# Gelu of 18 FFN tiles straight from PSUM and the attention normalisation on GpSimd, in a fused attention and FFN kernel

## The chip, the cores and the metric

The kernel runs on one core of a Trainium2 chip. The metric is the device time of one execution in microseconds (us). Engines are named as the profile names them: PE is TensorE's matmul, PEld its weight load, DVE VectorE, ACT ScalarE, POOL GpSimd, SP SyncE, which issues nearly all DMAs.

## The reference

The input x has 2048 rows of 512 in bf16. It is normalised per row (no gain or shift); on the result run a multi-query attention with 32 heads of width 16 that share one K and one V, and an FFN of width 1792. Their sum and x are the output.

```python
xn = (x - mean(x)) / sqrt(var(x) + 1e-5)
q = (xn @ wq) as 32 heads of 16;  k = xn @ wk;  v = xn @ wv      # one k and v for all heads
attn = (softmax(q k^T * 16**-0.5) @ v) @ wo
ffn = gelu_tanh(xn @ w1 + b1) @ w2 + b2                          # 512 -> 1792 -> 512
out = x + attn + ffn
```

## The kernel before

**Tiles and units.** The queries are cut into four blocks of 512 (`tb`), the heads into eight groups of four. A score tile is one head, one block of 128 keys and 512 queries: 128 x 512 fp32, one PSUM bank. There are 2048 of them, taken three at a time as 683 *units* `u`. `scores(u)` (L947) writes the unit's three tiles with three matmuls, side by side in PE's rows, into one half of six banks: banks 0 to 2 for even units, 3 to 5 for odd ones. Bank 6 (`pO`) holds the running sum of P x V, bank 7 (`pM`) whatever else is projected.

**Two ways to an exponential.** `DTAB` is a string with one letter for each unit and says which of its tiles are *D tiles*. The other tiles go to ACT: `exp(u)` (L970) writes E in bf16, one instruction for the one, two or three tiles of the unit, and one matmul sums each tile into `pO` (L1014, `E,V`). D tiles go to DVE: a first pass `p1` (L1001) reads the bank and writes the bits of an approximate exponential as int16 to `Dt`; then further passes make shifted copies, over a batch of several D tiles at a time (`close_batch`, L1047 on DVE), and one pass in place per tile on POOL (L1044, 128 x 512 int16), which the planner gives back to DVE where it finds no place. Five matmuls then sum a D tile (L1014, `Dt,V`). The column matmuls use 32 of PE's columns, so that four run side by side.

**FFN.** `h_mm` projects one of the 14 tiles of h of a query block into `pM` with 16 column matmuls (L661, `xnT,w_sb`), and DVE evacuates it with the bias b1 to `ub` (even blocks) or `x_sb` (odd ones) (L1150). Gelu needs another table on ACT than the exponential, so it is done in two batches: after units 182 and 512, for two query blocks at a time. `gelu` (L1162) issues four instructions of seven tiles each, 128 x 3584 in place in SBUF, between two table loads. The units near a batch are mostly D tiles. `y_mm` (L661, `w_sb,ub` and `w_sb,x_sb`) multiplies with w2 afterwards.

**Attention output.** After the last tile of a head group `o_evac` copies `pO` to `Of` on DVE (L1059). DMAs reorder it to `OfP`, the sums go through a reciprocal on DVE (L1071) and through DRAM to `rbP`, spread over the rows, and for each pair of groups DVE multiplies `OfP` by `rbP` into `oTp`, 128 x 512 from two fp32 inputs (L1086). `wo_mm` reads `oTp`.

**The order.** All instructions are recorded with a cost (`occ`) and a latency (`lat`). A planner at build time, `Prog.schedule`, lists them on the engines by those costs; what comes out is a fixed order for each engine, and the waits are semaphores. `HP`, `YP` and `QK` say at which unit an h tile, an output tile or a query projection is offered. The planner knows that a pass of POOL should not run beside DVE's `lock` instructions (passes of Dt, L1086): it starts POOL's together with a long DVE instruction that is not locked, and the constants `PL_START`, `PL_OCC`, `PL_LAT`, `PL_FREE`, `PL_SEM` say how. Where PE would idle too long in a stretch it adds filler matmuls (L1318).

Of the kernel before, what the change touches and what calls it, by code (L numbers as in the profile page):

```python
# [7 lines left out]
ALU = mybir.AluOpType  # L8
# [50 lines left out]
CLOSE = "otABX"  # L59
DTAB = "t2t22t00202t..22tt..022.to00.t22t00200..o.t..20222o.o2.tot22.2t.t2222tt22..2o222t2..o202o02tt2.o.2.t0.t202.2.20t0toto.2..0ot.t2..ot0o2t02t.2222o.0t...o0ot2020o2.2t0.02.t00.02.20o002..xxXaoto.02oot.0to2tt.0too0.ot0tot.o0o020t0o0.tt20.t22.o0tto..2t2to220oo.22t0.2ooo.o2t2o.0ot0o.t02t022.to0..oot.2t2t.o0002ot.0.2tto.0tt2.02t0.202t.2t.oo.ot0.00t.t0o0.0o0o..o0o22o2.00.t0tot2.0o2.2o.t2o2o.tt22o.0t.0oo.2ot2t2.o0.t0t20to2.2t0t.tt2t.002tt.oo.o0oooo0.2o0o0.t00t2ot2.0t0tt0.oA.o..020tt2t02..t0000...2o..02ot0020o.t2t...00XbXttto200t.tt0o22tt..0t0t222.o2o2.t2t20.t0t0.t0t00t2o.0tt2tot.t000202t2t.o.0to20.0.2o22t0o.2t00o0t0..t02o0.0o.o0ooto.t2t0to.2oo0o222o0022o00.2t.2..t0t2.2t.tttt2.2.to.o.."  # L60
YF = 664
# [11 lines left out]
HP = ((14.33,26.29,49.54,147.27,14,38.77,51.6,14,34.61,92.18,56.17,130.88,103.7,49),(108.69,82.59,66.39,104.08,133,93.7,109.35,162.93,173.36,139,171.29,159.02,133,137.17),(308.62,328.89,290.1,325,306.98,336.81,316.24,310.73,293.91,381.46,369.7,349,374.48,453.6),(475,473.57,427,468.62,459.3,464.72,451,455.66,491.16,486.09,482.33,480.6,464.72,461.37))  # L73
YP = ((195.26,184.23,228.93,254.61),(353.39,411.43,387.54,421),(516,530.79,566.23,553.42),(600.53,607,655.32,660.47))
GU = ((182, (0, 1)), (512, (2, 3)))
FG = 7
UB2 = 2
# [26 lines left out]
class _Op:  # L104
    __slots__ = ("eng", "fn", "deps", "sdeps", "stream", "amt", "need", "ticket", "waits", "clock", "occ", "lat",
                 "allow", "kind", "tag", "nun", "outs", "rel", "lock", "pm", "rdy", "start", "end", "vis", "idx", "done", "due", "real")


class Prog:
# [18 lines left out]

    def add(self, eng, fn, r=(), w=(), acc=None, dma=None, occ=0.1, lat=0.15, allow=1.0, kind=None, tag=None, after=(), due=None, lock=False):
        op = _Op()  # L130
        op.lock = lock
        op.eng, op.fn = eng, fn
# [46 lines left out]
        for o in after:  # L179
            sdeps.setdefault(id(o), (o, True))  # L180
        if self.in_chain:
# [42 lines left out]
    def schedule(self):  # L224
# [30 lines left out]
        started = {}  # L255
        opened = None
        lockend, gate, prev = 0.0, None, None
        s_seen = False
# [7 lines left out]
        while left:  # L266
# [71 lines left out]
            else:  # L338
# [26 lines left out]
                if e == "dve" and op.kind == "pl":  # L365
                    ready["pool"].remove(op)
                    ready["dve"].append(op)
                    op.eng = op.stream = "dve"
                    op.kind, op.occ, op.lat = "post", vcost(TBW, 4), 0.16
                if e == "dve":  # L370
# [86 lines left out]
    def settle(self):  # L457
        free = {e: 0.0 for e, _ in self.SECTIONS}
        mode, cg, pend = None, [0.0] * 4, 0.0
        for op in self.ops:  # L460
            occ = op.occ + EXP_OCC * (op.kind == "exp")
            lat = {"exp": EXP_LAT, "S": S_REAL, "fill": 0.0}.get(op.kind)
            lat = op.lat if lat is None else lat
            t = max([free[op.eng]] + [o.real for o in op.deps])
# [13 lines left out]
            free[op.eng] = max(free[op.eng], end)  # L478
            op.real = t + occ + lat

    def emit(self):
# [45 lines left out]
def bass_parallel_sum__grouped_kv_mqa__dense_activation_gelu__prompt_kernel(  # L527
# [33 lines left out]
    with ExitStack() as es:  # L561
# [80 lines left out]

        def dve(fn, r=(), w=(), n=TBW, mode=1, allow=1.0, lat=0.16, **kw):
            return add("dve", fn, r, w, occ=vcost(n, mode), lat=lat, allow=allow, **kw)

# [3 lines left out]
        def mm(o, l, rh, start, stop, r=(), w=(), tp=None, skip=False, occ=0.216, allow=1.5, **ak):  # L649
            kw = {}  # L650
            if tp is not None:
                kw["tile_position"] = tp
            if skip:
                kw["skip_group_check"] = True
            return add("pe", lambda e: e.matmul(o, l, rh, start=start, stop=stop, **kw), r, w, occ=occ, lat=0.23,  # L655
                       allow=allow, **ak)

        def mm4(o, l, rh, start, stop, r=(), w=(), allow=1.5, **ak):
            for j in range(4):
                c = slice(32 * j, 32 * j + 32)  # L660
                add("pe", lambda e, c=c, j=j: e.matmul(o[c, :], l[:, c], rh, start=start, stop=stop,  # L661
                                                       tile_position=(0, 32 * j)),
                    r, [(k, j) for k in w] + [k for k in w if k != B(7)], occ=0.216, lat=0.23, allow=allow, kind="side", tag=(None, j), **ak)

# [266 lines left out]
        exps = []  # L931

        def scores(u):
            ts = list(range(3 * u, min(3 * u + 3, NTILE)))
            x = u % 2
            pieces, r = [], []
# [17 lines left out]
        def exp(u):  # L954
            ts = list(range(3 * u, min(3 * u + 3, NTILE)))
            x = u % 2
            at_ = [i for i, t in enumerate(ts) if not is_d[t]]
# [55 lines left out]
        def pv_mm(gg, j, v, kt, rhs, r):  # L1013
            add("pe", lambda e, a, b: e.matmul(pO[32 * j:32 * j + 32, :], V1[:, v, kt, :], rhs, start=a, stop=b,  # L1014
                                               tile_position=(0, 32 * j)),
                r=r + [("V", v, 0 if kt < NVA else NVA)], acc="O", occ=0.216, lat=0.23,
                allow=4.0 if gg < NTB * NGR - 1 or kt < NT - 4 else -5.0, kind="pv", tag=(gg, j))

        def close_batch():
# [18 lines left out]
            for o, i, nb, k in SPL_STEPS:  # L1038
                def keys(b):
                    return [(("D", base[b + m > 0] + q), b + m) for m in range(nb) for q in range(n)]  # L1040
                if o == i:
                    for q in range(n):
                        d = Dt[:, slot(o) + q, :]
                        add("pool", lambda e, d=d, k=k: e.tensor_scalar(d, d, 1.0, float(k), ALU.mult, ALU.add),  # L1044
                            [], [(("D", base[o > 0] + q), o)], occ=PL_OCC, lat=PL_LAT, allow=PL_DUE, kind="pl", lock=True)
                else:
# [10 lines left out]
        def o_evac(gg):  # L1057
# [25 lines left out]
            if h or end:  # L1083
                n = 64 if end else P
                keys = [(k, s, hh, j) for k in ("OfP", "rbP") for hh in range(h + 1) for j in range(HG)]
                onorm[gg - h] = onorm[gg] = dve(lambda e: e.tensor_tensor(oTp[0:n, sl, :], OfP[0:n, s, :], rbP[0:n, s, :], ALU.mult),  # L1086
                                                r=keys, w=[("oTp", sl)] + pre.pop(sl, []), allow=3.0, lock=True)

# [57 lines left out]
        def h_mm(tb, ft, ev=EV_ALLOW):  # L1146
            for d in range(DT):
# [3 lines left out]
                r=["b1T"], w=M4 + [ukey(tb, ft)], n=TBW + 57, allow=ev)  # L1151

        gelu_after = {}

        def gelu(tbs, u):
            parts = [(tb, f0) for tb in tbs for f0 in range(0, FT, FG)]
            hold = exps[u - 3:u + 1]
            for n, (tb, f0) in enumerate(parts):
                uu = ubs[tb % 2][:, f0:f0 + FG, :]
                uk = [ukey(tb, f) for f in range(f0, min(FT, f0 + FG))]  # L1160
                load = 1.35 * (n == 0) + 1.35 * (n == len(parts) - 1)
                o = act(lambda e, uu=uu: e.activation(uu, uu, ACT.Gelu_apprx_tanh), r=uk, w=uk, n=len(uk) * TBW + 1200 * load + 40,  # L1162
                        kind="gelu", due=0.0, after=hold)
                hold = [o]
# [7 lines left out]
        def wo_mm(tb, i, ps, start=False, bk=7, al=1.5):  # L1172
            for n, p in enumerate(ps):
# [3 lines left out]
                mm4(bank(bk), oTp[:, pp % NPR, i * P:(i + 1) * P], wop[:, p, :], start and n == 0, False,  # L1177
                   r=[("oTp", pp % NPR), "wop"], w=[B(bk)], allow=al)

# [53 lines left out]
        for tb in range(NTB):  # L1233
# [6 lines left out]
            for ft in range(FT):  # L1240
                at(HP[tb][ft], lambda tb=tb, ft=ft: h_mm(tb, ft), 0.66)
            if tb + 1 < NTB:
# [16 lines left out]
        for t in range(NTILE):  # L1259
            if is_d[t]:  # L1260
                first, n = (t, 1) if n == 0 else (first, n + 1)
                if n == KB or last_d[t // TPG] == t or (DTAB[t // 3] in CLOSE and not any(is_d[t + 1:t // 3 * 3 + 3])):
                    bsize[first], n = n, 0

        scores(0)
        scores(1)
        for u in range(NU):
            ts = list(range(3 * u, min(3 * u + 3, NTILE)))
            exp(u)
            if u + 2 < NU:  # L1270
                scores(u + 2)
            for t in ts:
# [12 lines left out]
            if batch and len(batch) == size[0]:  # L1285
                close_batch()
            for gu, tbs in GU:
                if u == gu:
                    gelu(tbs, u)
            n0 = len(pr.ops)  # L1290
# [66 lines left out]
```

## Time and profile before

| | us |
|---|---|
| median of 3 runs | 750.98 (750.9 to 751.15) |
| profiled execution | 750.71 |
| its span, first to last instruction | 749.0 |
| DVE busy | 736.1 |
| ACT busy | 733.2 |
| PE busy | 732.8 |
| POOL busy | 364.4 |

A row of the grouped views has the line, engine, operation, out<-in by the program's names, shapes and the count; behind the bar the time in which one of the group ran, and the mean length of one in ns; behind the second bar the engine's idle time before them. A timeline row has the start in the span, the length, and the count of equal instructions that it merges. A row of stretches has the stretch, its length, and each engine's busy time with its instructions in brackets, then the granted clock, the DMA share and GB/s.

### The profile page before, as it was taken

The page shows a single profiled execution, that of the slowest core. Times are in us where ns is not written, and L with a number is a line of the kernel's source. Part 1 is how long each engine was busy: PE and PEld are TensorE (multiplying, and loading weights), DVE is VectorE, ACT ScalarE, POOL GpSimd, SP SyncE. Part 2 cuts the span into 40 slices and gives each one's busy share as a digit, 9 for nine tenths or more (in the row PEclk, how much of TensorE's full clock was granted, in tenths as well). Part 3 has the DMA queues.
Part 4 walks back from the last instruction along what each step waited for, and adds up shares of the span by engine and source line. Part 5 has one row for each costly group of instructions (what it writes and reads, how often), then busy time and mean ns, then how long its engine had stood idle before and what let it go on. Part 6 is the DMA issues. An engine that isn't in the chain of part 4 may idle for free.

```text
span 749.0 us, 21922 instructions
## 1 busy us (share of the span) xinstructions
PE 732.8 (98%) x9046; PEld 228.2 (30%) x9046; DVE 736.1 (98%) x1436; ACT 733.2 (98%) x744; POOL 364.4 (49%) x506
## 2 busy tenths in 40 slices
PE   7999999999999999999999999999999999999998
PEld 4323222222233323232222222332233333322223
DVE  8899999999999999999999999999999999999996
ACT  8999999999999999999999999999999999999995
POOL 5443654343523576554546555553452466454441
PEclk9999999999999999999999999999999999999999
DMA  9200100000011011100101010100100101010101
GB/s 315 61 15 17 32 9 17 24 11 21 6 36 25 9 39 30 24 23 16 26 13 28 17 38 19 29 24 16 25 15 22 40 6 41 23 39 10 25 22 37
DMA packets 32077, 23.34 MB, mean 31 GB/s; under 512 B 16369, under 2 KB 27498, under 8 KB 31978
## 3 DMA queue, kind: packets, MB, share of 16 engines
q1 hardware_dynamic: 30922, 21.90, 10.9%
q8 instruction: 72, 1.18, 0.7%
q14 instruction: 27, 0.22, 0.1%
q10 hardware_dynamic: 1056, 0.03, 0.1%
HBM read 13.08 MB, written 2.35 MB: 21 GB/s over the span
## 4 chain that ended last, share of the span: by engine, by line
PE 40%; DVE 30%; ACT 28%; DMA 0%; issue 0%; SPq 0%
ACT E L970 28%; PE pAll L1014 19%; DVE Dt L1001 13%; PE pAll L947 13%; DVE Dt L1047 10%; PE pAll L661 7%; DVE x_sb L1150 2%; DVE stats L748 1%; DVE Dt L1044 1%; DVE Of L1059 1%; PE pAll L655 1%; DMA x_sb<-in_A_x_dram 0%; DVE oTp L1086 0%; DVE qp L1122 0%; DVE x_sb L1196 0%
## 5 line engine op out<-in xcount | busy, mean ns | idle before, releaser
L970 ACT ACTIVATE E<-pAll 128x1024 bf16<-128x1024 f32 (+1 forms) x678 | 682.4, 1226 | 1.7 <-PE pAll L947 1.2
L1044 POOL TENSOR_SCALAR Dt<-Dt 128x512 int16<-128x512 int16 x451 | 348.2, 772 | 360.6 <-DVE Dt L1047 143.8
L1014 PE MATMUL pAll<-Dt,V 128*32 128x512 bf16 x2775 | 421.8, 383 | 0.6 <-DVE Dt L1047 0.2
L1001 DVE TENSOR_SCALAR Dt<-pAll 128x512 int16<-128x512 f32 (+1 forms) x542 | 364.1, 688 | 1.0 <-PE pAll L947 0.8
L1047 DVE TENSOR_SCALAR Dt<-Dt 128x1024 int16<-128x1024 int16 (+7 forms) x548 | 288.0, 551 | 0.2
L1014 PE MATMUL pAll<-E,V 128*32 128x512 bf16 x1493 | 284.8, 385 | 0.2
L947 PE MATMUL pAll<-QT,KT 32*128 32x512 bf16 x2048 | 267.2, 384 | 6.2 <-ACT E L970 2.1
L947 PEld LDWEIGHTS pAll<-QT,KT 32*128 32x128 bf16 x2048 | 67.3, 91 | 279.5 <-ACT E L970 251.4
L1014 PEld LDWEIGHTS pAll<-Dt,V 128*32 128x32 bf16 x2775 | 110.9, 94 | 119.4 <-issue 72.0
L661 PE MATMUL pAll<-xnT,w_sb 128*32 128x512 bf16 x896 | 122.2, 383 | 0.4 <-DVE x_sb L1150 0.3
L1014 PEld LDWEIGHTS pAll<-E,V 128*32 128x32 bf16 x1493 | 65.9, 94 | 47.5 <-issue 34.7
L661 PE MATMUL pAll<-w_sb,x_sb 128*32 128x512 bf16 x448 | 69.3, 383 | 0.0
L661 PE MATMUL pAll<-w_sb,ub 128*32 128x512 bf16 x448 | 69.3, 383 | 0.0
L661 PE MATMUL pAll<-wop,oTp 128*32 128x512 bf16 x256 | 49.5, 383 | 0.0
L661 PEld LDWEIGHTS pAll<-xnT,w_sb 128*32 128x32 bf16 x896 | 32.1, 95 | 22.4 <-issue 11.8
L1044 DVE TENSOR_SCALAR Dt<-Dt 128x512 int16<-128x512 int16 x104 | 26.7, 279 | 0.0
L661 PE MATMUL pAll<-xnT,wq_sb 128*32 128x512 bf16 x256 | 22.5, 383 | 0.0
L1150 DVE TENSOR_SCALAR x_sb<-pAll,b1T 128x512 bf16<-128x512 f32 x28 | 20.6, 736 | 0.7 <-PE pAll L661 0.6
L1059 DVE COPY Of<-pAll 128x512 f32<-128x512 f32 x31 | 20.9, 674 | 0.0
L1150 DVE TENSOR_SCALAR ub<-pAll,b1T 128x512 bf16<-128x512 f32 x28 | 20.6, 736 | 0.0
L661 PEld LDWEIGHTS pAll<-w_sb,x_sb 128*32 128x32 bf16 x448 | 17.1, 94 | 8.8 <-issue 7.0
L661 PEld LDWEIGHTS pAll<-w_sb,ub 128*32 128x32 bf16 x448 | 17.6, 94 | 4.7 <-issue 2.9
(121 smaller groups left out, 254.6 us busy)
## 6 DMA issues: line engine op xcount, KB each, us to landing
OfP<-Of SPq DMA_DIRECT2D x124, 32.0 KB, 1.9
rbP<-rden_rows SPq DMA_DIRECT2D x124, 32.0 KB, 1.8
w_sb<-in_B_w_dram SPq DMA_DIRECT2D x2, 1792.0 KB, 12.7
x_sb<-in_A_x_dram SPq DMA_DIRECT2D x8, 256.0 KB, 4.3
x_sb<-in_A_x_dram SPq DMA_DIRECT2D x16, 128.0 KB, 2.2
QT<-qp SPq DMA_DIRECT2D x124, 16.0 KB, 1.8
out_dram<-x_sb SPq DMA_DIRECT2D x12, 128.0 KB, 1.7
wq_sb<-in_A_wq_dram SPq DMA_DIRECT2D x1, 512.0 KB, 6.2
```

What stands on the lines that cost most here:

```text
L655: return add("pe", lambda e: e.matmul(o, l, rh, start=start, stop=stop, **kw), r, w, occ=occ, lat=0.23, allow=allow, **ak)
L661: add("pe", lambda e, c=c, j=j: e.matmul(o[c, :], l[:, c], rh, start=start, stop=stop, tile_position=(0, 32 * j)), r, [(k, j) for k in w] ...
L748: dve(lambda e, ti=ti, c=c: e.bn_stats(stats[:, c, :], x_sb[:, ti, :]), r=[("x", ti)], w=[("st", ti)], n=511, due=land(ti) + DU["sd"])
L947: ins = e.matmul(o, l, rh, start=True, stop=True, tile_position=(q0, 0))
L970: o = act(lambda e: e.activation(E[:, s0:s0 + na, :], bank(b0, na).rearrange("p (a n) -> p a n", a=na), ACT.Exp, scale=LN2 / 128.0), w=[B( ...
L1001: op = dve(lambda e: e.tensor_scalar(Dt[:, s:s + n, :], bank(bk, n).rearrange("p (a n) -> p a n", a=n), float(127 * 128) + SPL_D, SPL_MIN, ...
L1014: add("pe", lambda e, a, b: e.matmul(pO[32 * j:32 * j + 32, :], V1[:, v, kt, :], rhs, start=a, stop=b, tile_position=(0, 32 * j)), r=r + [ ...
L1044: add("pool", lambda e, d=d, k=k: e.tensor_scalar(d, d, 1.0, float(k), ALU.mult, ALU.add), [], [(("D", base[o > 0] + q), o)], occ=PL_OCC, ...
L1047: dve(lambda e, d=view(o, nb), q=view(i, nb), k=k: e.tensor_scalar(d, q, float(k), None, ALU.add), r=keys(i), w=keys(o), n=nb * n * TBW, m ...
L1059: dve(lambda e: e.tensor_copy(Of[:, i, :], pO), w=["O", ("Of", i)], allow=0.0)
L1150: dve(lambda e: e.tensor_scalar(ubs[tb % 2][:, ft, :], pM, b1T[:, ft:ft + 1], None, ALU.add), r=["b1T"], w=M4 + [ukey(tb, ft)], n=TBW + 57 ...
```

## The change

**Gelu.** Each batch keeps its two instructions of seven tiles on `ub`. Of the 14 tiles on `x_sb`, five are evacuated by DVE as before and pass through one instruction of 128 x 2560; the other nine ("p") are projected late: their 16 matmuls write into one of the three banks that the batch's unit has freed, and ACT reads the bank, adds b1 as its bias and writes gelu to `x_sb`, 128 x 512, with no DVE instruction. The order on ACT is 7 tiles of `ub`, three p, 7 of `ub`, three p, the five of `x_sb`, three p. While the batch runs the scores of the next units use the other half of the banks alone; `half[u]` replaces `u % 2`, and the next units' scores are offered when the half's last user is through.

**Normalisation.** L1086's product is cut in two halves of 256 columns, recorded for POOL like the passes of L1044 (the planner may give one back to DVE), and `wo_mm` waits for the half that it reads.

**Constants and tables.** The planner's costs and latencies change, and the visibility of an exponential or gelu is now modelled as a chain (`A_LAG`, `A_INC`, `A_SEM`). `DTAB` is another string: 565 D tiles rather than 555. `HP` and `YP` are new; the 18 p tiles have no due unit of their own.

```diff
+ON_OCC = 0.66
-PL_LAT = 0.2
+PL_LAT = 0.06
-PL_START = -0.07
+PL_START = 0.065
-PL_FREE = 0.135
+PL_FREE = 0.06
-DTAB = "t2t22t00202t..22tt..022.to00.
...
+DTAB = "o2t00o20.20.t0t.2.o2oot..0t0o
...
-S_LAT = 0.27
-S_REAL = 0.222
-EXP_OCC = 0.0133
-EXP_LAT = 0.16
+S_LAT = 0.217
+A_LAG = 0.113
+A_INC = 0.0125
+A_SEM = 0.056
+D_LAT = 0.135
+P_LAT = 0.217
...
-GU = ((182, (0, 1)), (512, (2, 3)))
-FG = 7
+GU = tuple((u, tbs, n, (("s", tbs[0], 0, 7), ("p", tbs[1], 5), ("p", tbs[1], 6), ("p", tbs[1], 7), ("s", tbs[0], 7, 7), ("p", tbs[1], 8),
+                         ("p", tbs[1], 9), ("p", tbs[1], 10), ("s", tbs[1], 0, 5), ("p", tbs[1], 11), ("p", tbs[1], 12), ("p", tbs[1], 13)))
+           for u, tbs, n in ((182, (0, 1), 5), (512, (2, 3), 5)))
+HL_ALLOW = 0.0
...
+            if e == "act" and op.kind in ("exp", "gelu"):
+                aend = max(op.end + A_LAG, aend + op.occ + A_INC)
+                op.vis = aend + A_SEM
...
+        half = []
+        for u in range(NU):
+            near = [gu for gu, _, n, _ in GU if gu + 1 < u <= gu + n]
+            half.append(u % 2 if u < 2 else half[-1] if near else 1 - half[-1])
...
-            x = u % 2
+            x = half[u]
...
-                onorm[gg - h] = onorm[gg] = dve(lambda e: e.tensor_tensor(oTp[0:n, sl, :], OfP[0:n, s, :], rbP[0:n, s, :], ALU.mult),
-                                                r=keys, w=[("oTp", sl)] + pre.pop(sl, []), allow=3.0, lock=True)
+                first = pre.pop(sl, [])
+                for q in range(2):
+                    c = slice(q * TBW // 2, (q + 1) * TBW // 2)
+                    onorm[gg - h] = onorm[gg] = add(
+                        "pool", lambda e, c=c: e.tensor_tensor(oTp[0:n, sl, c], OfP[0:n, s, c], rbP[0:n, s, c], ALU.mult),
+                        keys, [("oTp", sl, q)] + first, occ=ON_OCC, lat=PL_LAT, allow=PL_DUE, kind="pl", lock=True,
+                        docc=vcost(TBW // 2))
...
+        def h_late(tb, ft, bk):
+            for d in range(DT):
+                mm4(bank(bk), w1_sb[:, d, ft * P:(ft + 1) * P], xnT[:, d, tb * TBW:(tb + 1) * TBW], d == 0, d == DT - 1,
+                    r=["w1"] + tr(4 * tb, 4 * tb + 4), w=[B(bk)], allow=HL_ALLOW)
...
+            late = [p for p in parts if p[0] == "p"]
+            for i, (_, tb, ft) in enumerate(late[:3]):
+                h_late(tb, ft, 3 * half[u] + i)
...
+                else:
+                    bk = 3 * half[u] + m % 3
+                    o = act(lambda e, bk=bk, tb=tb, f0=f0: e.activation(ubs[tb % 2][:, f0, :], bank(bk), ACT.Gelu_apprx_tanh, bias=b1T[:, f0:f0 + 1]),
+                            r=["b1T"], w=[B(bk), ukey(tb, f0)], n=TBW + 1200 * load, kind="gelu", due=0.0, after=hold)
+                    m += 1
+                    if m + 2 < len(late):
+                        h_late(*late[m + 2][1:], bk)
```

More of the change, by code (lines that the diff above doesn't have):

```diff
@@ L105 @@
     __slots__ = ("eng", "fn", "deps", "sdeps", "stream", "amt", "need", "ticket", "waits", "clock", "occ", "lat",
-                 "allow", "kind", "tag", "nun", "outs", "rel", "lock", "pm", "rdy", "start", "end", "vis", "idx", "done", "due", "real")
+                 "allow", "kind", "tag", "nun", "outs", "rel", "lock", "pm", "rdy", "start", "end", "vis", "idx", "done", "due", "real", "docc")
 class Prog:
@@ L179, in add @@
         for o in after:
-            sdeps.setdefault(id(o), (o, True))
+            sdeps.setdefault(id(o), (o, kind != "gelu"))
         if self.in_chain:
@@ L479, in settle @@
             op.real = t + occ + lat
+            if op.kind in ("exp", "gelu"):
+                aend = max(end + A_LAG, aend + occ + A_INC)
+                op.real = aend + A_SEM
     def emit(self):
@@ L931, in bass_parallel_sum__grouped_kv_mqa__dense_activation_gelu__prompt_kernel @@
         exps = []
+        half = []
+        for u in range(NU):
+            near = [gu for gu, _, n, _ in GU if gu + 1 < u <= gu + n]
+            half.append(u % 2 if u < 2 else half[-1] if near else 1 - half[-1])
+        after_u = {}
+        for v in range(2, NU):
+            after_u.setdefault(max(w for w in range(max(0, v - 12), v) if half[w] == half[v]), []).append(v)
         def scores(u):
             ts = list(range(3 * u, min(3 * u + 3, NTILE)))
-            x = u % 2
+            x = half[u]
             pieces, r = [], []
@@ L1151, in h_mm, with gelu @@
                 r=["b1T"], w=M4 + [ukey(tb, ft)], n=TBW + 57, allow=ev)
+        def h_late(tb, ft, bk):
+            for d in range(DT):
+                mm4(bank(bk), w1_sb[:, d, ft * P:(ft + 1) * P], xnT[:, d, tb * TBW:(tb + 1) * TBW], d == 0, d == DT - 1,
+                    r=["w1"] + tr(4 * tb, 4 * tb + 4), w=[B(bk)], allow=HL_ALLOW)
         gelu_after = {}
-        def gelu(tbs, u):
-            parts = [(tb, f0) for tb in tbs for f0 in range(0, FT, FG)]
+        def gelu(parts, u):
             hold = exps[u - 3:u + 1]
[L1158 to L1163, printed above, removed]
+            late = [p for p in parts if p[0] == "p"]
+            for i, (_, tb, ft) in enumerate(late[:3]):
+                h_late(tb, ft, 3 * half[u] + i)
+            m = 0
+            for n, (kind, tb, f0, *k) in enumerate(parts):
+                load = 1.28 * (n == 0) + 1.28 * (n == len(parts) - 1)
+                if kind == "s":
+                    uu = ubs[tb % 2][:, f0:f0 + k[0], :]
+                    uk = [ukey(tb, f) for f in range(f0, f0 + k[0])]
+                    o = act(lambda e, uu=uu: e.activation(uu, uu, ACT.Gelu_apprx_tanh), r=uk, w=uk, n=len(uk) * TBW + 1200 * load + 50,
+                            kind="gelu", due=0.0, after=hold)
+                else:
[5 more added lines that the diff above has]
+                        h_late(*late[m + 2][1:], bk)
                 hold = [o]
@@ L1240, in bass_parallel_sum__grouped_kv_mqa__dense_activation_gelu__prompt_kernel @@
             for ft in range(FT):
-                at(HP[tb][ft], lambda tb=tb, ft=ft: h_mm(tb, ft), 0.66)
+                if ("p", tb, ft) not in [p for g in GU for p in g[3]]:
+                    at(HP[tb][ft], lambda tb=tb, ft=ft: h_mm(tb, ft), 0.66)
             if tb + 1 < NTB:
@@ L1269, in bass_parallel_sum__grouped_kv_mqa__dense_activation_gelu__prompt_kernel @@
             exp(u)
-            if u + 2 < NU:
-                scores(u + 2)
+            if u not in [g[0] for g in GU]:
+                for v in after_u.get(u, ()):
+                    scores(v)
             for t in ts:
@@ L1286, in bass_parallel_sum__grouped_kv_mqa__dense_activation_gelu__prompt_kernel @@
                 close_batch()
-            for gu, tbs in GU:
+            for gu, _, _, parts in GU:
                 if u == gu:
-                    gelu(tbs, u)
+                    gelu(parts, u)
+                    for v in after_u[u]:
+                        scores(v)
             n0 = len(pr.ops)
```

39 lines of the change are left out of this document (21 added, 18 removed).

## The prediction, made before the result was known

> **What bounds the kernel now.** I read the page's busy lines first, then a stretch without the ends, then what each engine waited for, and last the groups of instructions kept apart by shape.
>
> ```profile
> span 749.0 us, 21922 instructions
> ...
> PE 732.8 (98%) x9046; PEld 228.2 (30%) x9046; DVE 736.1 (98%) x1436; ACT 733.2 (98%) x744; POOL 364.4 (49%) x506
> ```
>
> ```profile
> 25.00:725.00 700.00, 693.46 (x8585) 208.98 (x8584) 698.65 (x1338) 697.47 (x678) 345.32 (x449) 1.00 0.09 22
> ```
>
> ```profile
> DVE x_sb L1150 <- PE pAll L661: 0.6, 1, 0.6
> DVE Dt L1001 <- PE pAll L947: 0.3, 1, 0.3
> ```
>
> Between 25 and 725 us PE, DVE and ACT are all busy for over 99% of the time (columns PE, PEld, DVE, ACT, POOL) at a granted clock of 1.00, and DVE's list of waits holds 0.9 us. Busy time alone can't tell which of the three paces: instructions overlap, and a short wait hides in the tail of the one before. So I work out what each instruction adds to a full engine.
>
> ```profile
> 216.35 0.74 DVE L1150 TENSOR_SCALAR x_sb<-pAll,b1T 128x512 bf16<-128x512 f32 x1
> 217.00 0.68 DVE L1001 TENSOR_SCALAR Dt<-pAll 128x512 int16<-128x512 f32 x1
> 217.60 0.34 DVE L1071 RECIPROCAL den<-den 128x32 f32<-128x32 f32 x1
> ```
>
> ```profile
> 19.71 0.68 ACT L818 ACTIVATE KT<-pAll,krow 128x512 bf16<-128x512 f32 x1
> 20.28 0.35 ACT L829 ACTIVATE oTp<-pAll 128x224 f32<-128x224 f32 x1
> 24.09 1.02 ACT L970 ACTIVATE E<-pAll 128x1024 bf16<-128x1024 f32 x1 [0.54 <-PE pAll L947]
> ```
>
> ```profile
> L970 ACT ACTIVATE E<-pAll 128x1024 bf16<-128x1024 f32 x535 | 519.8, 1139 | 0.8 <-PE pAll L947 0.5
> ...
> L970 ACT ACTIVATE E<-pAll 128x1536 bf16<-128x1536 f32 x140 | 214.5, 1571 | 0.9 <-PE pAll L947 0.7 <-PE pAll L1014 0.2
> ...
> L970 ACT ACTIVATE E<-pAll 128x512 bf16<-128x512 f32 x3 | 1.9, 629 | 0.0
> ```
>
> On DVE the next instruction starts 0.60 us after one of 0.68, and 0.65 after one of 0.74: an instruction costs its mean less 75 ns. Over all 1436 instructions of the grouped view that gives 735.2 us, against 736.1 busy: DVE has about 1 us of hidden waits. On ACT the next starts 0.57 after one of 0.68, an overlap of 0.11. An exponential of 1024 that starts on an idle engine lasts 1.02, so 0.91 in a row; one of 1536 is longer by 1571 - 1139 = 432 ns, so 1.34, one of 512 0.48. Sum: 535 x 0.91 + 140 x 1.34 + 3 x 0.48 = 676 us, where L970's union, by the page, is 682.4: some 6 us of ACT's busy time are waits. DVE is the fullest engine; ACT is close behind.
>
> PE runs score triples between groups of four column matmuls:
>
> ```profile
> 213.69 0.39 PE L947 MATMUL pAll<-QT,KT 32*128 32x512 bf16 x3
> 214.01 0.40 PE L1014 MATMUL pAll<-Dt,V 128*32 128x512 bf16 x4
> ...
> 217.14 1.04 PE L661 MATMUL pAll<-xnT,w_sb 128*32 128x512 bf16 x13
> ```
>
> Thirteen matmuls are four groups, so a group costs (1.04 - 0.38) / 3 = 0.22 us, with 0.38 the length of one. A triple costs 0.32 until the next work, and as much again less one group before it: some 0.42.
>
> **The change part by part.** Counts are those of the two built programs. The rows for DVE, ACT and POOL:
>
> ```profile
> L1001 DVE TENSOR_SCALAR Dt<-pAll 128x512 int16<-128x512 f32 x534 | 352.2, 675 | 1.0 <-PE pAll L947 0.8
> L1044 POOL TENSOR_SCALAR Dt<-Dt 128x512 int16<-128x512 int16 x451 | 348.2, 772 | 360.6 <-DVE Dt L1047 143.8 <-PE pAll L1014 93.6 <-DVE Dt L1001 46.2
> ...
> L1047 DVE TENSOR_SCALAR Dt<-Dt 128x1024 int16<-128x1024 int16 x204 | 82.2, 414 | 0.1
> L1047 DVE TENSOR_SCALAR Dt<-Dt 128x2048 int16<-128x2048 int16 x105 | 71.2, 680 | 0.0
> ...
> L1047 DVE TENSOR_SCALAR Dt<-Dt 128x3072 int16<-128x3072 int16 x44 | 41.4, 943 | 0.0
> ...
> L1047 DVE TENSOR_SCALAR Dt<-Dt 128x512 int16<-128x512 int16 x116 | 31.0, 278 | 0.0
> L1044 DVE TENSOR_SCALAR Dt<-Dt 128x512 int16<-128x512 int16 x104 | 26.7, 279 | 0.0
> ...
> L1047 DVE TENSOR_SCALAR Dt<-Dt 128x1536 int16<-128x1536 int16 x38 | 20.9, 549 | 0.0
> ...
> L1150 DVE TENSOR_SCALAR x_sb<-pAll,b1T 128x512 bf16<-128x512 f32 x28 | 20.6, 736 | 0.7 <-PE pAll L661 0.6
> L1047 DVE TENSOR_SCALAR Dt<-Dt 128x4096 int16<-128x4096 int16 x17 | 20.6, 1209 | 0.0
> ...
> L1047 DVE TENSOR_SCALAR Dt<-Dt 128x5120 int16<-128x5120 int16 x9 | 13.3, 1480 | 0.0
> ...
> L1162 ACT ACTIVATE x_sb<-x_sb 128x3584 bf16<-128x3584 bf16 x4 | 12.7, 3183 | 1.3 <-DVE x_sb L1150 1.3
> ...
> L1086 DVE TENSOR_TENSOR oTp<-OfP,rbP 128x512 bf16<-128x512 f32 x15 | 10.1, 676 | 0.0
> ...
> L1047 DVE TENSOR_SCALAR Dt<-Dt 128x2560 int16<-128x2560 int16 x9 | 7.3, 806 | 0.0
> ...
> L903 POOL TENSOR_SCALAR V<-oTp 128x256 bf16<-128x256 f32 x5 | 4.3, 866 | 5.9 <-DVE oTp L897 5.5
> ...
> L1114 DVE TENSOR_TENSOR oT<-Of,pAll 128x256 bf16<-128x256 f32 x2 | 0.8, 422 | 1.2 <-PE pAll L1110 1.2
> ...
> L702 POOL COPY oTp<-wvk 128x256 bf16<-128x256 bf16 x1 | 0.4, 406 | 0.0
> ```
>
> DVE loses 18 evacuations of h (L1150): 18 x 0.661 = 11.9. It loses 16 normalisations (L1086) of 0.601, 9.6, and keeps three half ones that the planner left there, 3 x 0.347 (L1114's row) = 1.0: net -8.6. It gains ten tiles in the new table: nine more single first passes, and two doubles for one triple, which is one more tile and is taken as a single, 10 x 0.600 = 6.0. Their later passes are regrouped: by width, 512 +7 x 0.203, 1024 -30 x 0.339, 1536 +5 x 0.474, 2048 -15 x 0.605, 2560 +5 x 0.731, 3072 +5 x 0.868, 4096 +5 x 1.134, 5120 +5 x 1.405, together +5.2. DVE: -11.9 - 8.6 + 6.0 + 5.2 = **-9.3 us**.
>
> ACT keeps 678 exponentials with ten tiles fewer: -10 x 0.432 = -4.3. Two gelus of 3584 start 3.09 us apart:
>
> ```profile
> 212.38 6.27 ACT L1162 ACTIVATE ub<-ub 128x3584 bf16<-128x3584 bf16 x2
> ```
>
> (6.27 - 3.18). Four such on x_sb go, -12.4. Two of 2560 come, each two times 0.432 shorter: +4.5. Eighteen of 512 straight from PSUM come, which the trace does not show. The nearest rows are an exponential of 512, 0.48, and L818, 512 from PSUM with a bias per partition as here, 0.57. I take L818's: 18 x 0.57 = +10.3 (8.6 by the other). ACT: -4.3 - 12.4 + 4.5 + 10.3 = **-1.9 us**, to -3.6.
>
> PE gets 50 more sums from Dt and 10 fewer from E, ten groups or +2.2 us, and 36 fewer filler matmuls (L1318), nine groups or -2.0. These are level; the h matmuls are the same number.
>
> POOL gets 29 half normalisations of 256 columns. Bounds are 0.41 (L702, one input, bf16) and 0.87 (L903, one fp32 input). A product has two fp32 inputs, so I take 0.7, nearer to L903: +20 us, less 7 x 0.77 of tile passes, on an engine with 384 us idle. The cover is that idle time. The new cost is order: a half waits for sixteen DMA landings (OfP and rbP of two head groups), and behind it in POOL's queue stand the tile passes (L1044) for whose sums PE waits. POOL's halves are also placed beside a first pass of 0.60 on DVE; a half of 0.7 would outlast it by 0.1, so 29 x 0.1 = 3 us if DVE's next pass must wait, nothing if it need not, 29 x 0.27 = 8 at L903's length. The row for L1044 lasts 772 on average while the same pass on DVE stands at 279 and the doubles at 414, with nothing in DVE's waits: so far POOL does the waiting, and I put 0 in the sum.
> The Trainium skill, GPSIMD Engine Reference, section 3.1, gives about 2.6 cycles an element for a product of two inputs at 1.2 GHz; an estimate from that is 256 x 2.6 / 1.2 = 0.55 us plus dispatch, inside my bounds; section 4.1 calls VectorE the engine for such work. No row here shows the product.
>
> The planner's constants and due times move only the static order. No row prices them; I put 0, with what the rivals give on either side.
>
> **The sum.** If DVE alone paced, the time would be 750.71 - 9.3 = 741.4; if ACT alone did, 750.71 - 1.9 = 748.8. Both serve the tiles in turn through two sets of three banks, so a wait of one is passed on to the other, and the total of idle time is likelier to stay than either one's. Then the gain is the mean of both, 5.6, and the time 745.1. The profiled execution took 750.71 (span 749.0 plus 1.7 around it); the median of the runs is 750.98, 0.27 above. I predict 745.4.
>
> **The rivals.** *ACT paces* (748.8): DVE's relief only becomes idle time. Against it: after the change DVE still has 726 us of work by the sum above, ACT some 725 (733.2 - 6 - 1.9). *DVE paces throughout* (741.4): ACT would have to lose nearly all of its hidden waits.
>
> *ACT waits for the late h tiles* (slower). A tile read straight from a bank must have its 16 matmuls, four groups or 0.88 us, done between the release of that bank and its gelu; ACT spends 0.57 on it.
>
> ```profile
> 211.08:226.75 15.67, 15.48 (x194) 5.45 (x191) 15.67 (x23) 15.12 (x7) 3.72 (x5) 1.00 0.16 34
> ```
>
> ```profile
> 211.08:226.75 15.67, 4.72 (x52) 1.68 (x52) 1.00 0.16 34
> ```
>
> These are the first gelu batch with its two table loads, and the fillers (L1318) alone in it: 52 matmuls were idle PE. In the new order the four score visits of this batch hold 244 other matmuls, 61 groups, 13.4 us, plus 4 x 0.42, 15.1 in all. ACT's new batch is 2 x 1.28 + 2 x 3.09 + 2.2 + 9 x 0.57 = 16.1. PE thus has 1 us of slack where it had fillers. In each batch the late tiles come in threes behind gelus of 3.1, 3.1 and 2.2 us; three tiles take PE 2.6, so the last three are not covered unless PE does little else. If each of the nine waits out half of its matmuls and some 0.3 of hand-over, 9 x 0.74 x 2 batches = 13 us; the forecast's gain is gone at 2.8 per batch. Taking half of the tiles, 6.7: 745.1 + 6.7 = 751.8. Also, one set of banks serves the scores meanwhile, without alternation.
>
> *POOL's halves hold DVE's passes* (750 to 755). The price above, 8 us on DVE, undoes its relief: 750.71 - (1.3 + 1.9) / 2 = 749.1; if each half blocked DVE for 0.7 without any cover, 20 us, 755. For it: the products read fp32 and no row shows them beside DVE; against it: L1044's rows.
> The Trainium skill, SBUF — State Buffer, section Who interferes with whom, has it that whichever of POOL and a two-port VectorE pass starts first holds their shared ports to its end; by that rule this rival is right wherever a half starts first.
>
> *The change does little* (750.7): the new table may be no better packed than the old one, and its ten tiles may take the relief elsewhere.
>
> **How the numbers follow.** Forecast, 742 to 748: 0.55. ACT paces: 0.12. DVE paces: 0.10. Late tiles: 0.11. POOL holds DVE: 0.07, of which half near no change. Little: 0.05. A measurement can tell about 0.2%, 1.5 us. Faster by more: the first three, 0.77; within: 0.06; slower: 0.17. The range, 741 to 751.5, takes in both pacing cases and the mild end of the slower ones, and leaves out under 0.2.
>
> **What would show it.** Right: L1150's x_sb group at 10 and 18 gelus of about 0.68 (0.57 in a row) from pAll; DVE's busy time down by 8 to 10 with small visible waits; batches of about 16 us; POOL up by some 15 us. Wrong: ACT idle before the gelus from pAll by over 1 us per group of three; DVE's doubles well over 414 on average; POOL among the first that PE waits for; or a DVE busy time that does not fall.

## The result and the profile after

The changed kernel takes 746.92 us (746.81 to 747.11, four runs) beside 750.94 (750.81 to 751.15): a ratio of 0.9947, interval 0.9934 to 0.9959, 4.0 us or 0.5% faster. The profiled execution took 747.11, its span is 745.3, 3.7 less than before. The page's span and busy lines, the stretch from 25 to 725 us, and all that DVE and ACT visibly wait for in it:

```profile
span 745.3 us, 21947 instructions
...
PE 729.3 (98%) x9050; PEld 222.9 (30%) x9050; DVE 730.7 (98%) x1402; ACT 730.1 (98%) x760; POOL 380.7 (51%) x528
```

```profile
25.00:725.00 700.00, 692.78 (x8642) 203.95 (x8640) 697.25 (x1313) 698.32 (x697) 362.62 (x473) 1.00 0.09 23
```

```profile
DVE Dt L1022 <- PE pAll L968: 2.1, 5, 0.8
```

```profile
ACT E L991 <- PE pAll L968: 2.0, 4, 0.5
```

DVE's busy time fell by 5.4 us, ACT's by 3.1, POOL's rose by 16. ACT is now the busier of the two in the stretch, and DVE's first passes (L1022) wait for scores (L968) where they hardly did. The page's chain that ended last (shares of the span, followed back from the last instruction), first before and then after, says the same:

```profile
PE 40%; DVE 30%; ACT 28%; DMA 0%; issue 0%; SPq 0%
```

```profile
ACT 75%; PE 21%; DVE 3%; DMA 1%; issue 0%; SPq 0%
```

The groups that the change made or shortened (shapes kept apart; count, busy us, mean ns):

```profile
L1022 DVE TENSOR_SCALAR Dt<-pAll 128x512 int16<-128x512 f32 x543 | 362.1, 680 | 2.8 <-PE pAll L968 2.1
...
L1069 DVE TENSOR_SCALAR Dt<-Dt 128x1024 int16<-128x1024 int16 x174 | 71.2, 416 | 0.1
...
L1065 DVE TENSOR_SCALAR Dt<-Dt 128x512 int16<-128x512 int16 x121 | 32.0, 282 | 0.0
...
L1112 POOL TENSOR_TENSOR oTp<-OfP,rbP 128x256 bf16<-128x256 f32 x28 | 22.5, 812 | 12.7 <-DVE Dt L1069 9.2 <-DVE Dt L1022 1.6 <-DVE Of L1081 0.7
...
L1202 ACT ACTIVATE x_sb<-pAll,b1T 128x512 bf16<-128x512 f32 x18 | 11.1, 701 | 0.0
...
L1177 DVE TENSOR_SCALAR x_sb<-pAll,b1T 128x512 bf16<-128x512 f32 x10 | 7.4, 742 | 0.0
L1198 ACT ACTIVATE x_sb<-x_sb 128x2560 bf16<-128x2560 bf16 x2 | 4.7, 2366 | 0.0
```

The first gelu batch on ACT (timeline):

```profile
209.26 1.28 ACT L1198 ACT_TABLE_LOAD   x1
210.56 3.19 ACT L1198 ACTIVATE ub<-ub 128x3584 bf16<-128x3584 bf16 x1
213.66 1.82 ACT L1202 ACTIVATE x_sb<-pAll,b1T 128x512 bf16<-128x512 f32 x3
215.36 3.19 ACT L1198 ACTIVATE ub<-ub 128x3584 bf16<-128x3584 bf16 x1
218.44 1.85 ACT L1202 ACTIVATE x_sb<-pAll,b1T 128x512 bf16<-128x512 f32 x3
220.15 2.37 ACT L1198 ACTIVATE x_sb<-x_sb 128x2560 bf16<-128x2560 bf16 x1
222.38 1.87 ACT L1202 ACTIVATE x_sb<-pAll,b1T 128x512 bf16<-128x512 f32 x3
224.27 1.28 ACT L991 ACT_TABLE_LOAD   x1
225.56 4.69 ACT L991 ACTIVATE E<-pAll 128x1024 bf16<-128x1024 f32 x5
```

It runs without a visible wait from the start of the first table load to the next exponential, 16.30 us (225.56 - 209.26). The three late tiles of a group start 0.56 to 0.59 apart: (1.82 - 0.70) / 2 for the first group, (1.87 - 0.70) / 2 for the last. Before, each of the two batches had one visible wait for DVE's evacuations; after, this line of ACT's waits is gone:

```profile
ACT x_sb L1162 <- DVE x_sb L1150: 1.3, 2, 0.7
```

**A finer measure.** Since short waits hide in busy time, I took from the traces the time from each instruction's start to the next start on its engine, and subtracted the lower quartile of the same for its form; what is over 25 ns counts as a wait, the rest as work. From the first exponential to the last but one:

```
kernel         DVE work  waits    ACT work  waits
before           706.1    5.0       701.0   11.4
after            697.0    9.3       698.4   10.2
```

DVE's work fell by 9.1 and its waits rose by 4.3. ACT's work fell by 2.6, its waits by 1.2, and that sum, 3.8, is the gain. The 1.2 are the two gelu waits for evacuations (1.2 by this measure too); ACT's other waits stayed, 10.2 before and after. The measure depends somewhat on where the stretch is cut and how forms are grouped: taken otherwise, DVE's work falls by 8.4 and ACT's by 3.1, and the waits come out up to 0.5 us different. Where a run has shortened exponentials, most of them have a wait right behind them, so their form's lower quartile is taken from the kernels without them; by the run's own quartile ACT's waits there would come out some 9 us lower.

**Where in the span it is gained.** The start of the scores of a unit in the two traces, and how many more D tiles the new table has had up to there:

| unit | start before, us | lead of the changed kernel, us | more D tiles so far |
|---|---|---|---|
| 0 | 24 | -0.4 (behind) | 0 |
| 180 | 207 | 0.7 | 4 |
| 200 | 240 | 1.4 | 7 |
| 340 | 380 | 1.0 | 5 |
| 480 | 520 | 0.8 | 2 |
| 520 | 576 | 4.3 | 11 |
| 680 | 736 | 3.6 | 10 |

The lead does not grow steadily with DVE's relief. It grows where the new table takes tiles from ACT, above all around the second gelu batch, and shrinks a little where it gives tiles back. That fits ACT as the pace, but it is read from two traces and was not tested by a run.

### The profile page after: what moved, and what is told of

Read it like the earlier page. It is cut to its first block, busy times and chain, and to the rows that moved or that the text cites. A ratio compares the mean times of both kernels' runs of the same rounds, so it can differ in the third digit from the quotient of the medians.

```text
span 745.3 us, 21947 instructions
## 1 busy us (share of the span) xinstructions
PE 729.3 (98%) x9050; PEld 222.9 (30%) x9050; DVE 730.7 (98%) x1402; ACT 730.1 (98%) x760; POOL 380.7 (51%) x528
## 4 chain that ended last, share of the span: by engine, by line
ACT 75%; PE 21%; DVE 3%; DMA 1%; issue 0%; SPq 0%
ACT E L991 70%; PE pAll L1035 10%; PE pAll L968 7%; PE pAll L674 4%; ACT ub L1198 2%; ACT x_sb L1202 1%; DVE Dt L1022 1%; PE pAll L668 1%; DVE stats L761 1%; ACT x_sb L1198 1%; DMA x_sb<-in_A_x_dram 1%; DVE Dt L1069 0%; ACT L991 0%; ACT L1198 0%; PE pAll L812 0%; ACT xnT L817 0%
## 5 line engine op out<-in xcount | busy, mean ns | idle before, releaser
L1065 POOL TENSOR_SCALAR Dt<-Dt 128x512 int16<-128x512 int16 x444 | 340.3, 766 | 326.8 <-DVE Dt L1069 136.3
L1022 DVE TENSOR_SCALAR Dt<-pAll 128x512 int16<-128x512 f32 (+1 forms) x552 | 374.9, 693 | 2.8 <-PE pAll L968 2.1
L1069 DVE TENSOR_SCALAR Dt<-Dt 128x1024 int16<-128x1024 int16 (+6 forms) x518 | 290.8, 585 | 0.2
L968 PE MATMUL pAll<-QT,KT 32*128 32x512 bf16 x2048 | 267.2, 385 | 6.6 <-ACT E L991 4.1
L1035 PE MATMUL pAll<-E,V 128*32 128x512 bf16 x1483 | 272.1, 384 | 0.1
L968 PEld LDWEIGHTS pAll<-QT,KT 32*128 32x128 bf16 x2048 | 66.6, 91 | 288.4 <-ACT E L991 274.0
L1035 PEld LDWEIGHTS pAll<-Dt,V 128*32 128x32 bf16 x2825 | 108.8, 94 | 115.3 <-issue 76.8
L674 PE MATMUL pAll<-xnT,w_sb 128*32 128x512 bf16 x896 | 111.3, 382 | 0.9 <-ACT x_sb L1202 0.9
L674 PE MATMUL pAll<-wop,oTp 128*32 128x512 bf16 x256 | 46.1, 383 | 0.0
L1065 DVE TENSOR_SCALAR Dt<-Dt 128x512 int16<-128x512 int16 x121 | 32.0, 282 | 0.0
L1112 POOL TENSOR_TENSOR oTp<-OfP,rbP 128x256 bf16<-128x256 f32 (+1 forms) x29 | 23.9, 831 | 13.7 <-DVE Dt L1069 9.2
```

The source lines that it names most:

```text
L968: ins = e.matmul(o, l, rh, start=True, stop=True, tile_position=(q0, 0))
L1022: op = dve(lambda e: e.tensor_scalar(Dt[:, s:s + n, :], bank(bk, n).rearrange("p (a n) -> p a n", a=n), float(127 * 128) + SPL_D, SPL_MIN, ...
L1069: dve(lambda e, d=view(o, nb), q=view(i, nb), k=k: e.tensor_scalar(d, q, float(k), None, ALU.add), r=keys(i), w=keys(o), n=nb * n * TBW, m ...
L1112: "pool", lambda e, c=c: e.tensor_tensor(oTp[0:n, sl, c], OfP[0:n, s, c], rbP[0:n, s, c], ALU.mult),
```

## Experiments

All were timed beside the kernel before. Except for the last, the planner sees the old costs, so that each kernel runs the same instruction order as the one it is made from, with some instructions added, shortened or moved. The changed kernel was timed in the first session only (746.92); in the sessions of the experiments the kernel before lay between 750.80 and 751.02, so differences from 746.92 are uncertain by some 0.2.

**Added work: which engine paces.** A dummy behind every twentieth unit's exponential on ACT, or behind every sixteenth first pass on DVE:

```diff
+                    if u % 20 == 10:
+                        e.activation(dscr[:], epsc[:, 0:1].to_broadcast([P, 256]), ACT.Exp)
...
+                if k % 16 == 8:
+                    e.memset(dscr[:], 0.0)
```

> The changed kernel with some 33 activations of 256 fp32 columns on ACT, one behind the exponential of every twentieth unit, in an order that is otherwise the same; about 0.3 us each, 10 us in all. Theory: after the change ACT is the engine that paces, since DVE got 9 us lighter and ACT 2, so 8 us or more of the 10 reach the time (755 or more). Rival A: the two engines share the pace as before, and about half reaches it (752). Rival B: PE's hand-over of scores paces, and under a third reaches it (750 or less).

> The changed kernel with 34 memsets of 256 fp32 columns on DVE, one behind every sixteenth first pass, order otherwise the same; about 0.27 us each, 9 us in all. Theory: DVE now has slack of some 5 us that is spread, so about half of the 9 reaches the time (751 to 752). Rival A (DVE still paces): 8 or more (755). Rival B: under a third (750 or less).

> The kernel before with the same activations on ACT, 10 us. Theory: before, DVE paced and ACT had some 6 us of hidden waits and 2 of visible ones, so about half or less reaches the time (754 to 756). Rival (ACT paces, DVE's relief was worth nothing): 8 or more (759).

> The kernel before with the same memsets on DVE, 9 us. Theory: DVE had 1 us of hidden waits, so 8 or more reaches the time (759 or more). Rival (the two share the pace): about half, 755.

The sizes first, from the timelines of the changed kernel with the one and with the other:

```profile
34.53 0.49 ACT L997 ACTIVATE dscr<-epsc 128x256 f32<-128x256 f32 x1
34.83 2.02 ACT L994 ACTIVATE E<-pAll 128x1024 bf16<-128x1024 f32 x2
```

```profile
33.27 0.27 DVE L1029 MEMSET dscr<- 128x256 f32 x1
33.48 0.48 DVE L1077 TENSOR_SCALAR Dt<-Dt 128x1536 int16<-128x1536 int16 x1
```

34 activations add 0.305 us each, 10.4. A memset lasts 0.27, and the next instruction starts 0.19 to 0.20 after it, so 35 of them add 6.6 by that measure (34 of them 6.7 in the kernel before). Compared in place with the kernels without them, the memset's two neighbours start 0.27 further apart, but the two intervals behind them are together 0.07 shorter, so 0.20 is left, 6.9 and 6.8 in all, not the 9 that I had expected.

| | added, us | time | above its own base | share |
|---|---|---|---|---|
| after, ACT | 10.4 | 756.50 | +9.6 | 92% |
| after, DVE | 6.6 | 748.76 | +1.8 | 28% |
| before, ACT | 10.4 | 758.70 | +7.8 | 75% |
| before, DVE | 6.7 | 756.40 | +5.5 | 82% |

(Bases: 746.92 and 750.95. By 6.9 and 6.8 DVE's shares are 27% and 80%.) After the change ACT paces, as the theory had it, and DVE has slack for 4.8 of the 6.6. Before, the theory was wrong about ACT: both engines passed on most of what was added, so both paced; ACT did not have the spare time that I read from the profile.

**Work taken away.** The 18 evacuations that the change takes from DVE, shortened in the kernel before; one exponential in each twentieth unit shortened in either kernel (the columns and the tile that are left out are not computed at all):

```diff
+            c = slice(0, 32 if tb % 2 and ft >= 5 else TBW)
-            dve(lambda e: e.tensor_scalar(ubs[tb % 2][:, ft, :], pM, b1T[:, ft:ft + 1], None, ALU.add),
+            dve(lambda e: e.tensor_scalar(ubs[tb % 2][:, ft, c], pM[:, c], b1T[:, ft:ft + 1], None, ALU.add),
...
+                nx = 1 if u > 60 and u % 20 in (10, 11, 12) and na == 2 and u // 20 * 20 not in short else na
+                if nx < na:
+                    short.add(u // 20 * 20)
-                o = act(lambda e: e.activation(E[:, s0:s0 + na, :], bank(b0, na).rearrange("p (a n) -> p a n", a=na),
+                o = act(lambda e: e.activation(E[:, s0:s0 + nx, :], bank(b0, nx).rearrange("p (a n) -> p a n", a=nx),
```

> The kernel before, with 18 evacuations of h (those that the change takes from DVE) reduced from 512 to 32 columns, so that DVE is lighter by 18 x 0.5 = 9.0 us, as much as the change makes it, with ACT's work and every order kept; the rest of those h columns is not computed. Theory: the relief counts until ACT, which has 6 to 8 us of waits, paces: -3 to -4.5 (746.5 to 748), nearly the whole gain of the change. Rival (the share of 82% that added work on DVE had holds downward): -7.4 (743.5). Rival (the gain of the change is ACT's relief alone): under -1.5 (749.5 or more).

> The kernel before, with one exponential of 1024 in every twentieth unit reduced to 512 columns, 31 x 0.43 = 13 us less on ACT, order kept; one score tile in 66 is not computed anew. Theory: DVE, which has no slack, paces at once: -2 to -4 (747 to 749). Rival (both share the pace, half counts): -6.5 (744.5).

> The changed kernel with the same 13 us less on ACT. Theory: ACT paces now and DVE has some 9 us of waits, so more counts than in the kernel before: -5 to -8 (739 to 742). Rival (the share of 92% that added work had holds downward): -12 (735). Rival (DVE or PE paces as soon): -3 or less (744 or more).

| | taken away, us | time | against its base | ratio to before |
|---|---|---|---|---|
| before, DVE | 9.0 | 749.06 | -1.7 | 0.9978 (0.9968 to 0.9987) |
| before, ACT | 13 | 749.79 | -1.0 | 0.9987 (0.9978 to 0.9996) |
| after, ACT | 13 | 742.58 | -4.3 | 0.9891 (0.9877 to 0.9906) |

The first is the main finding: DVE's relief alone, as large as the change's, is worth 1.7 us, less than the theory's 3 to 4.5. DVE's waits in the stretch from 25 to 725 us show where most of it went, into waiting for scores, 3.1 us beside 0.3 before:

```profile
DVE Dt L1001 <- PE pAll L947: 3.1, 12, 0.5
DVE x_sb L1151 <- PE pAll L661: 0.4, 1, 0.4
```

What it did gain lies almost wholly in two places. Compared instruction by instruction on ACT, the last gelu of the first batch starts 0.61 us sooner after the one before it, that of the second batch 0.84; these 1.45 are the waits for DVE's evacuations shown above, which are gone. All the rest of the relief brought some 0.4 from the first exponential on.

By the finer measure DVE's waits there rose from 5.0 to 12.3 while ACT's fell from 11.4 to 9.6 only. With ACT relieved instead, DVE's stayed at 4.6 and ACT's rose to 22.9. So it looks as if neither engine comes below a floor of waits in these orders: some 9.4 us on ACT (9.6 here, 9.5 and 9.3 with work added to ACT), some 4.8 on DVE (5.0 before, 4.6). The room of an engine is its waits above that floor:

| | room of ACT | room of DVE |
|---|---|---|
| before | 11.4 - 9.4 = 2.0 | 5.0 - 4.8 = 0.2 |
| after | 10.2 - 9.4 = 0.8 | 9.3 - 4.8 = 4.5 |

Added work costs what exceeds its engine's room; work taken away gains until the other engine's room is used up. For the seven runs this gives (measured in brackets): after, ACT +9.6 (9.6); after, DVE +2.1 (1.8); before, ACT +8.4 (7.8); before, DVE +6.5 (5.5); before, DVE less -2.0 (1.7); before, ACT less -0.2 (1.0); after, ACT less -4.5 (4.3). The floors are fitted to some of these runs; the next ones are not. Two things weaken the rule: 1.2 of ACT's 2.0 before are the two gelu waits, which only evacuations can free; and with the memsets in the kernel before DVE's waits come down to some 3.6, under the floor (a first pass takes 0.08 longer to the next start where a memset follows, and that is not counted as waiting here).

**PE.** The score triple of every sixteenth unit issued twice:

```diff
-                for o, l, rh, q0 in pieces:
+                for o, l, rh, q0 in pieces * (2 if u % 16 == 8 else 1):
```

> The changed kernel with the score triple of every sixteenth unit issued twice, 42 x 0.22 = 9.1 us more on PE in front of the exponential that waits for it, order otherwise the same. Theory: PE stands between ACT's banks and DVE's sums and has little slack; a third to two thirds counts (750 to 753). Rival (PE's hand-over of scores paces): 8 or more (755). Rival (PE has slack, the waits are in ACT and DVE alone): under 2 (749 or less).

749.30, +2.4, a ratio of 0.9981 (0.9971 to 0.9990 against the kernel before): about a quarter of the 9 us (43 triples took 0.216 longer), under the theory's range. PE is not the pace, but not free either: ACT's waits rose to 12.3, 2.9 above the floor.

**The normalisation, moved back at fixed order.** After the planner has set the changed kernel's order, the 29 halves on POOL are handed to DVE at the same places:

```diff
-                        docc=vcost(TBW // 2))
+                        docc=vcost(TBW // 2), tag="on")
...
         pr.schedule()
+        for op in pr.ops:
+            if op.tag == "on":
+                op.eng = op.stream = "dve"
```

> The changed kernel in its own planned order, but with the 29 half normalisations of POOL issued by DVE at the same places: DVE +29 x 0.35 = 10 us, POOL -24. Theory: DVE's added work passes on 28% as the memsets' did: +2.8 (749.7), so this part of the change is worth nearly 3 us. Rival (POOL's halves held DVE up or came late): +1 or less (748). Rival (a normalisation stands where DVE has no wait to fill): 5 or more (752).

The halves on DVE (shapes kept apart):

```profile
L1112 DVE TENSOR_TENSOR oTp<-OfP,rbP 128x256 bf16<-128x256 f32 x30 | 13.0, 434 | 0.1
```

752.72, +5.8; slower than the kernel before at 1.0023 (1.0014 to 1.0033). By that mean the 29 added cost (434 - 75) ns each, 10.4 us; from start to next start most take 0.33 to 0.34, which makes 9.7. Less DVE's room of 4.5 this gives +5.2 to +5.9. The theory's 28% gave +2.8 and was wrong. The room fits here, but the run does not prove it: by the finer measure DVE keeps some 6.6 us of waits, not 4.8, and the rival (a normalisation stands where DVE has no wait to fill) named 5 or more and fits as well. In this order the move to POOL is worth more than the whole gain of the change; that does not show POOL's halves to be free, only that they cost less than the same work on DVE.

**Both reliefs together, in the kernel before.** The 18 shortened evacuations, with five or 31 shortened exponentials:

```diff
-                nx = 1 if u > 60 and u % 20 in (10, 11, 12) and na == 2 and u // 20 * 20 not in short else na
+                nx = 1 if u > 60 and u % 120 in (10, 11, 12) and na == 2 and u // 120 not in short else na
```

> The kernel before with both reliefs of the size of the change, order kept: the 18 evacuations reduced to 32 columns (DVE -9.0) and five exponentials of 1024 reduced to 512 columns (ACT -2.1); those columns and tiles are not computed anew. Theory: ACT paces and DVE's relief alone gave -1.7, so the two add up: -1.7 - 0.75 x 2.1 = -3.3 (747.5), most of the change's -4.0, and the new order brings the rest. Rival (only joint relief counts, ACT's waits shrink too): -4 to -5.5 (745.3 to 746.8). Rival (the new order and table bring the gain, not the reliefs): -2.2 or less (748.6 or more).

> The same with 31 shortened exponentials, DVE -9.0 and ACT -13. Alone the two gave -1.7 and -1.0. Theory: each engine stopped at the other, so together they give far more than the sum of the two: -6 to -9 (742 to 745). Rival (PE or the fixed order paces): the sum, about -2.8 (748).

748.52 (0.9967, 0.9954 to 0.9980), -2.5, and 747.06 (0.9948, 0.9931 to 0.9964), -4.0. The two rooms would have given -4.1 and -9. Here the rule of floors fails: with both reliefs large, DVE keeps 10.4 us of waits and ACT 20.3. Both wait for PE's scores (stretch 25 to 725, DVE's list, then ACT's):

```profile
DVE Dt L1005 <- PE pAll L948: 2.6, 10, 0.4
```

```profile
ACT E L974 <- PE pAll L948: 4.6, 16, 0.7
```

So reliefs of the change's size, put into the old order, bring 2.5 of its 4.0 us, of which the two gelu waits are again 1.45. What is left, 1.5, belongs to the new order and the new table, or to where in the span the reliefs lie: the shortened evacuations all stand ahead of or in the two gelu batches, and the new table takes its ten tiles from ACT unevenly (seven by unit 200, five fewer from there to unit 480, nine more by 520). I did not separate these two. Nor is it settled whether PE's work or the fixed order holds the last kernel.

**The constants alone.** Three planner constants of the changed kernel, in the kernel before, with its old table:

```diff
-PL_LAT = 0.2
+PL_LAT = 0.06
-PL_START = -0.07
+PL_START = 0.065
-PL_FREE = 0.135
+PL_FREE = 0.06
```

> The kernel before with three of the new planner constants alone (PL_LAT 0.06, PL_START 0.065, PL_FREE 0.06) and its old table, so that the planner lays out another order. In that order 77 tile passes more fall back from POOL to DVE (181 on DVE instead of 104), 77 x 0.20 = 15 us, and PE gets 208 filler matmuls instead of 136. Theory: a table holds only for the constants with which it was chosen, so the constants can't be judged alone: at the 82% of added work on DVE, +13 or more (764 or more). Rival (the constants describe the chip better and the order gains by itself): -2 (749). Rival (they change nothing that matters): within 1 (750 to 752).

782.71, +31.8 (1.0424, 1.0379 to 1.0469). The tile passes and what ACT waits for in the middle stretch:

```profile
L1044 DVE TENSOR_SCALAR Dt<-Dt 128x512 int16<-128x512 int16 x181 | 46.9, 294 | 0.0
```

```profile
ACT E L970 <- PE pAll L1014: 12.9, 10, 2.7
ACT E L970 <- PE pAll L947: 9.4, 10, 4.4
ACT x_sb L1162 <- DVE x_sb L1150: 7.8, 3, 5.2
```

Theory's sign, and over twice its least size: beside the 77 passes on DVE ACT waits visibly for 30 us, mostly for PE. The table is chosen for one set of constants. For this reason no other part of the change was tried alone with a fresh plan, and the constants' own worth stays open: they can only be had together with a table.

## Why the prediction was right, and where it was off

The sign and the range hold; the mechanism holds in part. The forecast was -5.6, the result -4.0. The range reached from 741 to 751.5 and so took in no change at all; that it held is no strong test.

- **The counts and prices.** DVE -9.3 was forecast, -9.1 measured. ACT -1.9 was forecast, -2.6 measured by the finer measure. DVE's busy time fell by 5.4, not by the 8 to 10 that were to show it, since most of its new waits hide in the tails that count as busy. The price of the late gelus was right: L818's 0.57 was taken, 0.56 to 0.59 measured, and the batch took 16.30 where 16.1 was worked out. The Trainium skill, ScalarE: Activation LUTs, section What ACT_TABLE_LOAD costs, gives 280 ns + 0.833 ns a column for an activation with a bias per partition, and about 93 ns of overlap between activations in a row. An estimate from that is 0.71 us for 512 columns and 0.61 in a row; the trace's 701 ns agrees with the first, its 0.56 to 0.59 are a little under the second.
- **The step that failed** is "the total of idle time is likelier to stay than either one's. Then the gain is the mean of both, 5.6". It did not stay: DVE's waits rose by 4.3 us and ACT's fell by 1.2, so the total rose by 3.1, and half of that, 1.6, is what the forecast had too much. What DVE was relieved of beyond ACT's own gain became idle time, as the rival "ACT paces" had it. But ACT gained more than its work: the prediction's own row for L1162 shows 1.3 us of waiting for DVE's evacuations, which the change removes, and the sum has no term for it. "ACT paces" with that term would have been 750.71 - 1.9 - 1.3 = 747.5 beside 747.11 measured for the profiled execution. The forecast rested on reading ACT's 6 us of hidden waits as spare time that DVE's relief would free. The kernel with DVE alone relieved shows that it frees hardly any: -1.7, of which 1.45 are the two gelu waits. After the change, work added on ACT reached the time by 92%.
- **Luck.** The forecast came near because it averaged the two pacing cases, not because idle time was kept. Why ACT's other 10.2 us of waits stay is not shown.
- **"DVE is the fullest engine; ACT is close behind"** was half right. Added work on ACT passed on 75% in the kernel before: two engines can pace at once.
- **Late h tiles:** no visible wait in ACT's batch, although by the prediction's count the order left PE only 1 us of slack; the three-tile groups start right behind the gelus that cover them, the last one too.
- **POOL holds DVE:** it does not. In the trace after, the doubles last 416 ns (414 before) and the single passes on DVE 282 (279); DVE waits for scores, not for passes of its own. A half on POOL lasts 718 ns at the least and 812 on the mean, over the 0.7 that was taken: POOL does the waiting. Of the 29 halves twelve start beside first passes or evacuations alone and last 0.72 to 0.73; ten start some 0.16 us into a Dt pass of 1024 and last 0.83 to 0.84, three in one of 512 0.73, and four in longer passes 1.10 to 1.37. By the Trainium skill, SBUF — State Buffer, section Who interferes with whom, a half that starts first would hold a two-port pass. No row shows this here: no Dt pass starts in a half before its last 0.1 us.
- **PE level:** its matmuls are as forecast, 100 fillers against 136. That some waits for scores stay on both others whatever is relieved was not in the prediction. PE in turn waits visibly for ACT to free a bank (4.1 us between 25 and 725), so who sets these waits is not shown.

## What to carry to other kernels

Where several engines are busy for 99%, price a relief by adding and taking away known work on each engine at fixed order, not by busy time: a relief is worth no more than the waits of the other engine that it removes, and not all waits go. A relief of 9 us on one of two pacing engines was worth 1.7 alone, nearly all of it in two waits that a row of the profile had named. A change to the inputs of a planner whose table was searched for can't be judged without a new table: three constants alone cost 32 us.

## What the runs showed of the hardware that was not expected

A first pass of 0.68 on DVE is followed 0.60 later by the next instruction, but by a memset only 0.68 later: the memset did not overlap its tail in any of the 69 places. The memset itself (128 x 256 fp32) lasts 0.27, and the next instruction starts 0.19 to 0.20 after it. On ACT an activation of 256 columns that lasts 0.42 at the least adds 0.305. The product of two fp32 inputs, 128 x 256, takes 0.72 us at the least on POOL (mean 0.81); on DVE it takes 0.43 on the mean, and in a row mostly 0.33 to 0.34.
